# Twelve matmuls on four banks ahead of the last x, and another order of SyncE and GpSimd in one batch, in a fused attention + GELU MLP kernel

## Chip, cores, metric

One core of a Trainium2 chip. The metric is device microseconds of one execution; medians of several executions are quoted.

## The reference, cut

```python
B, H, S, D = 8, 8, 576, 64
scores = q @ k.T / sqrt(D);  cum = cumsum(log(clip(f, 1e-4, 1)))
scores = where(causal, -1e9, scores + cum[:, None] - cum[None, :])
attn   = softmax(scores) @ v                    # (B, H, S, D)
x      = attn.transpose(0, 2, 1, 3).reshape(B * S, 512)
out    = gelu(x @ w_in) @ w_out                 # w_in 512x2048, w_out 2048x512, float32 out
```

## The kernel before

The kernel runs batch by batch. In the attention of batch b (b >= 2) TensorE interleaves score tiles (`scores`), the attend matmuls of the head pair before (`av`) and steps of the second GEMM of batch b-1 (`take(fill, n)`). A step is "n" (one matmul of 128 rows) or "r" (two of 64 rows that run side by side). Each head pair's x is normalized on VectorE and transposed into xT by a DMA that SyncE issues (`x_dma`). The first GEMM of the batch then contracts over xT in four parts `kt`, one for each head pair; `kt = 3` needs the last x, which comes last.

```python
PLAN_1 = [(0, "m", 14*"r" + 2*"n"), (1, "m", 14*"r" + 2*"n"),
          (2, "m", 14*"r" + 2*"n"), (3, "s", 6*"r" + 10*"n")]     # second GEMM of batch 1, run in batch 2
FILL   = [[7,6,3,3], [1,3,3,2], [1,3,3,3], [1,3,3,3], [6]]        # steps taken after each score tile
FILL_2 = [[8,8,8,8], [8,8,4,4], [4,4,4,4], [4,4,4,4], [6]]        # the same for batch 2

def attention(b):
    ...
    for i in range(HP):                       # head pairs
        for t in range(4):                    # score tiles: matmuls, exp on ScalarE, masks on GpSimd
            scores(b, i, t)
            take(fill, counts[i][t])
            if i and t == 1:
                av(i - 1)                     # attend + normalize
                x_dma(b, i - 1)               # SyncE: transpose x -> xT
            if t == 1 and i == 0:
                load_v(b + 1)                 # SyncE: 5 DMAs into v_sb, once its last reader is done
            if b > 2 and t == 0 and i < 2:
                transpose_dma(b + 1, 4 * i, 4 * i + 4)
            if b == 2 and t == 1 and i == 1:
                transpose_dma(3, 0, 4)        # SyncE: q and k of the next batch
                transpose_dma(3, 4, 8)
    take(fill, counts[HP][0])
    av(HP - 1)
    x_dma(b, HP - 1)
    take(fill, 999)

    pss = [gemm1(b, ffb, (0, 1)) for ffb in range(2)]       # 4 matmuls
    for ffb in range(2):
        gemm1(b, ffb, (2,), pss[ffb])                       # 2
    pss.append(gemm1(b, 2, (0, 1, 2), spare()))             # 3: nine ahead of the last x
    for ffb in range(3):
        gemm1(b, ffb, (3,), pss[ffb])
    gemm1(b, 3, range(4), spare())
    ...
# in the rest of the first GEMM of batch 1: GpSimd computes vw = v * w for the pairs of batch 2
    if late == gap - 2:
        weigh_v(b + 1, at)                    # two instructions, about 1.4 us on GpSimd
```

The softmax here doesn't subtract the row's maximum and nothing guards it: scores larger than these inputs give would overflow.

## Time and profile before

| | before |
|---|---|
| median, first three executions | 346.34 us |
| median of six, with the later ones | 345.51 us (344.77 to 346.74) |
| profiled execution | 345.78 us, span 343.7 us |
| TensorE busy | 97% of the span |
| undisturbed first GEMM of a batch | 64 matmuls in 13.81 us |

The span is what the trace covers; the time of the execution is some 2 us longer. The prediction shows the lines that bound the kernel. How to read them: the chain lists the work that ended last, so where it leaves TensorE, TensorE stood.

### The profile page before, as it was taken

The numbers are of one execution on the slowest core, as the hardware profiler recorded it, in microseconds if no ns is written. First come the engines' busy times: TensorE is split into PE (matmuls) and PEld (weight loads), VectorE is DVE, ScalarE is ACT, GpSimd is POOL, SyncE is SP. The second block draws the span as 40 slices with busy tenths as digits, with TensorE's granted clock in tenths as the row PEclk, the third lists the DMA queues.
The fourth block names the chain that finished last, engine by engine and source line by source line (L and its number), as shares of the span: only waits on it lengthen the run. The fifth ranks groups of instructions, "written<-read, shape, count | busy, mean of one in ns | idle before, by whom it ended". The sixth has DMA issues, their size and how long they took to land.

```text
span 343.7 us, 7855 instructions
## 1 busy us (share of the span) xinstructions
PE 332.7 (97%) x3180; PEld 172.4 (50%) x3180; DVE 183.1 (53%) x417; ACT 210.4 (61%) x296; POOL 125.4 (36%) x256
## 2 busy tenths in 40 slices
PE   7899999999998999999999999999999999999995
PEld 3574555445553456445644465446544554444443
DVE  5660455943357934796469646975497551020011
ACT  5986786773743687378737873687568765504600
POOL 8391572219333334443436243714450430000000
PEclk9999999999999999999999999999999999999999
DMA  8999999989996799769973998299910131011013
GB/s 117 177 158 191 208 180 137 167 174 144 220 174 171 111 166 191 152 85 158 212 162 42 174 194 175 45 177 201 180 44 2 52 101 50 0 63 62 0 34 90
DMA packets 104628, 44.18 MB, mean 129 GB/s; under 512 B 83408, under 2 KB 100048, under 8 KB 104592
## 3 DMA queue, kind: packets, MB, share of 16 engines
q1 hardware_dynamic: 87296, 29.52, 44.2%
q0 software_dynamic: 16896, 13.63, 27.0%
q8 instruction: 25, 0.41, 0.5%
q10 hardware_dynamic: 400, 0.52, 0.4%
q14 instruction: 11, 0.09, 0.1%
HBM read 36.85 MB, written 9.44 MB: 135 GB/s over the span
## 4 chain that ended last, share of the span: by engine, by line
PE 88%; DMA 4%; DVE 2%; POOL 2%; ACT 2%; issue 1%; SPq 0%; POOLq 0%; ACTq 0%
PE ps L375 34%; PE ps L469 26%; PE o L320 8%; PE ps L411 8%; PE s L289 7%; DMA xT<-x 2%; PE ps L504 2%; ACT e L299 2%; DMA k<-in_k_dram 2%; POOL q L107 1%; PE ps_f L206 1%; DVE x L334 1%; POOL k L107 1%; PE ps_x L353 1%; DVE r L333 0%
## 5 line engine op out<-in xcount | busy, mean ns | idle before, releaser
L395 ACT ACTIVATE g<-ps 128x512 bf16<-128x512 f32 x144 | 83.4, 598 | 83.4 <-PE ps L375 82.9
L299 ACT ACTIVATE e<-s 128x896 bf16<-128x896 f32 (+2 forms) x128 | 101.2, 836 | 28.5 <-PE s L289 26.8
L375 PE MATMUL ps<-xT,w_in_sb 128*128 128x512 bf16 x512 | 113.3, 379 | 1.9 <-DMA xT<-x 1.8
L469 PE MATMUL ps<-w_out_sb,g 64*128 64x512 bf16 (+1 forms) x744 | 109.2, 377 | 0.0
L375 PEld LDWEIGHTS <-w_in_sb 128*128 128x128 bf16 x576 | 55.9, 98 | 70.2 <-issue 5.1
L301 POOL TENSOR_SCALAR_AFFINE_SELECT e<-e 128x256 bf16<-128x256 bf16 (+1 forms) x135 | 49.4, 384 | 94.6 <-ACT e L299 94.3
L469 PEld LDWEIGHTS <-g 64*128 64x128 bf16 (+1 forms) x744 | 41.7, 94 | 41.7 <-issue 11.9
L260 POOL TENSOR_TENSOR vw<-v_sb,wT 128x640 bf16<-128x640 f32 x31 | 39.9, 1288 | 34.2 <-DMA v_sb<-in_v_dram 24.7
L289 PE MATMUL s<-qT,kT 64*128 64x320 bf16 (+4 forms) x384 | 45.8, 276 | 3.4 <-ACT e L299 2.7
L477 DVE COPY ot<-ps 128x512 f32<-128x512 f32 x26 | 18.0, 691 | 48.0 <-PE ps L469 48.0
L244 DVE COPY kT<-tk 64x288 bf16<-64x288 bf16 x96 | 42.1, 438 | 1.6
L244 DVE COPY qT<-tq 64x288 bf16<-64x288 bf16 x96 | 38.9, 405 | 1.4
L320 PEld LDWEIGHTS <-e 128*128 128x128 bf16 x960 | 34.8, 98 | 5.8 <-issue 0.6
L320 PE MATMUL o<-vw,e 128*128 128x65 bf16 x960 | 36.9, 194 | 0.3 <-POOL e L301 0.2
L334 DVE TENSOR_TENSOR x<-o,r 128x320 bf16<-128x320 f32 x64 | 31.4, 491 | 2.2
L420 DVE COPY ot<-ps 128x512 f32<-128x512 f32 (+2 forms) x9 | 5.7, 632 | 48.9 <-PE ps L411 48.9
L289 PEld LDWEIGHTS <-kT 64*128 64x128 bf16 x384 | 19.5, 94 | 23.1 <-issue 9.7
L411 PE MATMUL ps<-w_out_sb,g 128*128 128x512 bf16 (+2 forms) x144 | 28.0, 355 | 0.0
L333 DVE RECIPROCAL r<-o 128x5 f32<-128x5 f32 x64 | 12.1, 189 | 25.0 <-PE o L320 24.9
L411 PEld LDWEIGHTS <-g 128*128 128x128 bf16 x144 | 13.5, 98 | 14.5
L479 DVE TENSOR_TENSOR ot<-ot,ps 128x512 f32<-128x512 f32 x26 | 17.8, 686 | 1.4
L375 PE MATMUL ps<-tails,w_in_sb 128*128 128x512 bf16 x64 | 14.4, 378 | 0.0
(64 smaller groups left out, 139.6 us busy)
## 6 DMA issues: line engine op xcount, KB each, us to landing
out_dram<-ot SPq DMA_DIRECT2D x32, 256.0 KB, 2.5
v_sb<-in_v_dram SPq DMA_DIRECT2D x24, 256.0 KB, 5.1
q<-in_q_dram POOLq DMA_DIRECT2D x6, 576.0 KB, 6.2
k<-in_k_dram POOLq DMA_DIRECT2D x6, 576.0 KB, 8.6
v_sb<-in_v_dram SPq DMA_DIRECT2D x22, 128.0 KB, 5.4
w_in_sb<-in_moe_w_in_dram POOLq DMA_DIRECT2D x4, 512.0 KB, 7.1
w_out_sb<-in_moe_w_out_dram POOLq DMA_DIRECT2D x4, 512.0 KB, 8.4
q<-in_q_dram POOLq DMA_DIRECT2D x4, 144.0 KB, 4.6
```

The lines of the kernel that those rows point to most:

```text
L244: nc.vector.tensor_copy(rows[:, odd], src[odd * D : (odd + 1) * D, 2 * i + h].rearrange("d j p -> d p j"),)
L260: eng.tensor_tensor(vw_of[b][:, hs, :, 0:D], v_sb[:, hs, :, :], w.unsqueeze(3).to_broadcast([P, 2, NBLK, D]), Alu.mult,)
L289: nc.tensor.matmul(to, *ab, start=half < 0, stop=half == 1 or not masked)
L299: nc.scalar.activation(et[:, :, z:c], st[:, :, z:c], Act.Exp, scale=scale)
L301: nc.gpsimd.affine_select(out=et[:, :, c0 + z : c0 + P], in_=et[:, :, c0 + z : c0 + P], compare_op=Alu.is_ge, fill=0.0, base=z, pattern=[[ ...
L320: nc.tensor.matmul(o[:, m, :], e_of[b, i, t][:, h, c : c + P], vw_of[b][:, 2 * i + h, n, :], start=(n == 0), stop=(n == m),)
L334: nc.vector.tensor_tensor(x_of[b, i][:, :, h, :], o[:, :, 0:D], r.unsqueeze(2).to_broadcast([P, NBLK, D]), Alu.mult,)
L375: nc.tensor.matmul(ps, w_in_sb[:, kt, ffb * P : (ffb + 1) * P], src[:, kt, 0:TC], start=(kt == 0), stop=(kt == n_dm - 1),)
L395: nc.scalar.activation(g_of[c][ffb], ps, Act.Gelu)
L411: nc.tensor.matmul(pss[ts][:, c0:c1], g_of[c][kt][:, ts * P : (ts + 1) * P], w_out_sb[:, kt, c0:c1], start=(kt == 0), stop=(kt == n_ff - 1),)
L469: nc.tensor.matmul(banks[r], g_of[c][kt][rows, ts * P : (ts + 1) * P], w_out_sb[rows, kt, :], start=kt == (steps.index("r") if r else 0), ...
L477: nc.vector.tensor_copy(ot, banks[1])
```

## The change

Three intents. First, every opening of the first GEMM in batches 2 to 7 gets more work that doesn't need the last x: twelve matmuls on four banks (each tile of the first GEMM adds up its four parts in one bank) in place of nine on three, and one second-GEMM step (two in batch 2) moves behind the last attend. Second, in batch 2 the q/k transposes of heads 4 to 7 go behind the last x in SyncE's queue, and two of the four products of v go behind the masks of the first head pair on GpSimd, with the next v load behind them. Third, the plan of the second GEMM that runs in batch 2 ends in whole steps only. The core of the diff:

```diff
-        (2, "m", 14 * "r" + 2 * "n"),
-        (3, "s", 6 * "r" + 10 * "n"),
+        (2, "m", 12 * "r" + 4 * "n"),
+        (3, "s", 16 * "n"),
...
-    FILL = [..., [6]];  FILL_2 = [..., [6]]
+    FILL = [..., [5]];  FILL_2 = [..., [4]]
...
-                if t == 1 and i == 0:
+                if b == 2 and (i, t) == (0, 3):
+                    weigh_v(b, 2)
+                    weigh_v(b, 3)
+                if i == 0 and t == (3 if b == 2 else 1):
                     load_v(b + 1)
...
                     transpose_dma(3, 0, 4)
-                    transpose_dma(3, 4, 8)
...
         x_dma(b, HP - 1)
+        take(fill, 4)
+        if b == 2:
+            transpose_dma(3, 4, 8)
         take(fill, 999)
...
-        pss.append(gemm1(b, 2, (0, 1, 2), spare()))
-        for ffb in range(3):
+        pss += [gemm1(b, ffb, (0, 1, 2), spare()) for ffb in (2, 3)]
+        for ffb in range(4):
             gemm1(b, ffb, (3,), pss[ffb])
-        gemm1(b, 3, range(4), spare())
+        more = s_psum.tile([P, 2, 512], FP32, tag="s", name="ps1")
+        gemm1(b, 4, ps=more[:, 0, :])
...
-                if late == gap - 2:
+                if late == gap - 2 and (b > 1 or at < 2):
                     weigh_v(b + 1, at)
```

(Cut: the copy-out of a tile without "r" steps, one VectorE copy in place of a copy and an add, and the numbering of the later tiles.)

More of the change, by code (lines that the diff above doesn't have):

```diff
@@ L465, in gemm2_rows @@
             for kt, step in enumerate(steps):
-                last = kt == steps.rindex("r")
+                last = kt == steps.rfind("r")
                 for r in range(2 if step == "r" else 1):
@@ L475, in gemm2_rows @@
                     )
-                if kt == n_ff - 1 if held == "s" else last:
+                if "r" in steps and (kt == n_ff - 1 if held == "s" else last):
                     nc.vector.tensor_copy(ot, banks[1])
                 if kt == n_ff - 1:
-                    nc.vector.tensor_tensor(ot, ot, banks[0], Alu.add)
+                    if "r" in steps:
+                        nc.vector.tensor_tensor(ot, ot, banks[0], Alu.add)
+                    else:
+                        nc.vector.tensor_copy(ot, banks[0])
                     store(c, ts, ot)
@@ L616, in gemm1_begin @@
         gelu(b, 3, pss[3])
-    FILL = [[7, 6, 3, 3], [1, 3, 3, 2], [1, 3, 3, 3], [1, 3, 3, 3], [6]]
-    FILL_2 = [[8, 8, 8, 8], [8, 8, 4, 4], [4, 4, 4, 4], [4, 4, 4, 4], [6]]
+    FILL = [[7, 6, 3, 3], [1, 3, 3, 2], [1, 3, 3, 3], [1, 3, 3, 3], [5]]
+    FILL_2 = [[8, 8, 8, 8], [8, 8, 4, 4], [4, 4, 4, 4], [4, 4, 4, 4], [4]]
     FILL_1 = [[0, 0, 0, 0], [0, 0, 0, 0], [2, 2, 2, 2], [2, 2, 2, 2]]
@@ L716 @@
             x_tail(0)
-        for ffb in range(4, n_ff):
-            gemm1(b, ffb, ps=spare() if b > 1 and ffb in (6, 7) else None)
+        for ffb in range(4 if b < 2 else 5, n_ff):
+            gemm1(b, ffb, ps=spare() if b > 1 and ffb in (7, 8) else None)
             if b == 0:
@@ L729 @@
             elif b + 1 < B:
-                first, gap = (5, 3) if b == 1 else (0, 4)
+                first, gap = (5, 3) if b == 1 else (1, 4)
                 at, late = divmod(ffb - first, gap)
```

## The prediction

> **What bounds the kernel now.** I read the page's busy shares first, then the chain that ended last, then the waits of TensorE, then the timeline around each place where that chain leaves TensorE. Page, part 1 (engine, busy us, share, instructions):
>
> ```profile
> PE 332.7 (97%) x3180; PEld 172.4 (50%) x3180; DVE 183.1 (53%) x417; ACT 210.4 (61%) x296; POOL 125.4 (36%) x256
> ```
>
> Only TensorE is near its span, and its clock row shows 9 in all 40 slices, so no throttle plays. A busy share says nothing on headroom where matmuls overlap, so the pitch matters. The chain in order of time (start us, length us, what) shows three openings of the first GEMM (L375), 64 matmuls each:
>
> ```profile
> 105.76 2.60 DMA xT<-x
> 108.40 12.03 PE ps L375 x55
> ...
> 142.01 13.81 PE ps L375 x64
> ...
> 176.18 3.40 DMA xT<-x
> 179.61 12.03 PE ps L375 x55
> ...
> 212.68 2.60 DMA xT<-x
> 215.32 12.03 PE ps L375 x55
> ...
> 248.93 13.81 PE ps L375 x64
> ```
>
> An undisturbed batch (3, 6, 7) is one piece of 64 matmuls in 13.81 us: 215.8 ns each. In batches 2, 4 and 5 the chain passes through the DMA transpose that brings x into xT, and only 55 matmuls follow it: the nine that can run without the last x were done, and TensorE stood. The list of TensorE's waits makes that the only sizeable one after batch 1:
>
> ```profile
> PE s L289 <- ACT e L299: 2.7, 7, 0.5
> PE ps L375 <- DMA xT<-x: 1.8, 4, 1.2
> ```
>
> (total us, times, longest. The first lies in the first two batches, which the change leaves alone.) The 1.8 understates it, since a matmul's modelled end (379 ns) overlaps the next; I work with starts. TensorE at the opening of batch 2:
>
> ```profile
> 104.52 0.38 PE L375 MATMUL ps<-xT,w_in_sb 128*128 128x512 bf16 x1
> 105.12 0.81 PE L375 MATMUL ps<-xT,w_in_sb 128*128 128x512 bf16 x3 [0.22 <-DMA xT<-x]
> 107.08 3.21 PE L375 MATMUL ps<-xT,w_in_sb 128*128 128x512 bf16 x13 [1.15 <-DMA xT<-x]
> ```
>
> Nine matmuls from 104.52 at 0.2158 end at 106.46; the tenth began at 108.40 (chain). **Batch 2 loses 1.94 us**: 0.38 before the second matmul (x of head pair 1), 1.31 before the fifth (pair 2), 0.24 before the tenth (pair 3). In batch 4 the first starts at 177.24, so the tenth could start at 179.18 and did at 179.61: **0.43 us**. Batch 5: 213.06, 215.00, 215.32: **0.32 us**. Together 2.69 us.
>
> Why is batch 2 different? SyncE's own timeline (start, length of the issue, what):
>
> ```profile
> 82.67 9.11 SPq L119 DMA_DIRECT2D v_sb<-in_v_dram  x5
> 91.83 1.09 SPq L484 DMA_DIRECT2D out_dram<-ot  x2
> 93.11 1.28 SPq L359 DMA_TRANSPOSE xT<-x  x1
> 94.47 1.36 SPq L230 DMA_TRANSPOSE tq<-q  x1
> 95.92 1.66 SPq L230 DMA_TRANSPOSE tk<-k  x1
> 97.64 2.13 SPq L230 DMA_TRANSPOSE tq<-q  x1
> 99.82 1.69 SPq L230 DMA_TRANSPOSE tk<-k  x1
> 101.61 0.76 SPq L484 DMA_DIRECT2D out_dram<-ot  x1
> 102.47 1.23 SPq L359 DMA_TRANSPOSE xT<-x  x1
> ```
>
> SyncE issues in order. The load of the next v occupies it for 9 us, four q/k transposes of the next batch for 7 more, and x of pair 1, whose last normalize ended near 91.7 (its attend matmuls ended near 90.6, plus about 1.1 us on VectorE as in the later batches), is not issued before 102.47. Pairs 2 and 3 follow at 104.42. So it is the queue's order that is late, not the data.
>
> **What the Trainium skill says.** "TensorE: Matmul & The Clock Gate", section "Wait — 56ns, not 53.3ns?": warm matmuls of 512 columns start 215.7 ns apart. The trace agrees (13.81 us / 64 = 215.8). "Perfetto Trace Analysis", section "Summary: the profiler window per engine type": the window of a DMA issued by SyncE covers the lock wait, descriptor generation and the semaphore push, not the data movement. So the lengths above are time for which the queue is held, and the landing comes on top; the DMA list gives 2.7 us median from issue to landing for x. "DMA: Bandwidth & Descriptors", section "Issuing engines are not separate DMA queues": queues of all issuers run on the same 16 engines and interleave. The trace agrees: the v load held SyncE for 9.11 us while q and k were still loading, against 4.93 us in batch 3, after k had landed. "TensorEngine Tiling (Array Packing)", section "Key Properties": switching the tiling mode drains TensorE. In batch 2, 18 steps of the second GEMM with two changes of mode took 104.52 - 100.43 = 4.09 us against 18 x 0.2158 = 3.88, so about 0.1 us a change.
>
> **Part 1: twelve matmuls and one more step.** The opening goes from nine matmuls ahead of the last x to twelve: 3 x 0.2158 = 0.65 us more cover in batches 2 to 7, by putting the fourth tile of d_ff ahead too. In batches 3 to 7 the attend of the last pair moves one second-GEMM step earlier and that step runs after it: 0.22 us more. Cover grows by 0.86 us, the work stays the same. Against needs of 0.43 (batch 4) and 0.32 (batch 5) both waits should go: **0.75 us** saved. In batches 3, 6 and 7 there is nothing to win.
>
> **Part 2: SyncE in batch 2.** Two of the four q/k transposes (the 2.13 and 1.69 us, 3.9 with gaps) go behind the x of pair 3. Against that, the v load is emitted two score tiles later and waits for the two products of v on GpSimd, which now come after the masks of pair 0. The last exponential of pair 0 ends at 82.77 + 0.81 = 83.6; its mask takes 0.4 at most, to 84.0; the two products 1.28 + 0.23 each with gaps, to about 86.9. So the v load starts near 86.9 instead of 82.67. By then q and k, issued at 78.4, should be nearly in: in batch 3 they were issued at 113.20 and k had landed by 123.3, 10 us, hence 88.5 here. I take 5.5 us for the five issues (4.93 when alone): free at 92.4, 0.6 later than now. From there by the row lengths above: one store 0.5, x of pair 0 1.3, two transposes 3.1, a store 0.8, x of pair 1 issued at about 98.3, landed 101.0; a store, x of pair 2 issued near 100.2, landed 102.9; x of pair 3 once its normalize ends.
> The attend of pair 3 starts two steps earlier (0.43 us), so that end is 101.52 - 0.43 = 101.1; issued by 102 it lands by 104.7. The first GEMM starts near 104.3 and needs pair 1 at 104.5, pair 2 at 105.2 and pair 3 at 104.3 + 12 x 0.2158 = 106.9. All in time: **1.94 us** saved.
>
> **Part 3: plan of batch 2.** The last tile is now sixteen whole steps and the tile before it ends in four, so after the attend there is no change of mode until the first GEMM: two changes less, **0.2 us**. VectorE saves one copy of 0.69 us, off the path.
>
> **Part 4: the banks.** A fifth tile takes a bank pair of the score pool. Its earlier user is read by the exponential that ended by 98.2 in batch 2, long before. Four tiles now finish within 0.86 us, and ScalarE needs 0.60 us each: done 2.65 us after the first. The sixth tile takes the first tile's bank 1.73 us after that end, free since 0.6; the ninth comes back to the fourth's bank at 4.3, free since 2.65. No wait added.
>
> Sum: 0.75 + 1.94 + 0.2 = 2.9 us; 346.34 - 2.9 = 343.4. The profiled run, whose waits I sized, took 345.78, a little under the median, so the median run may have lost somewhat more: I say **343.3**.
>
> **Rivals.** (a) SyncE stays late in batch 2. If the v load again takes 9.1 us from 86.9 it frees the queue at 96.0, pair 1 is issued near 101.9, lands at 104.6, pair 2 at 106.5 against 105.2, pair 3 near 107.9. About 1.3 us of the 1.94 comes back: 344.7. For it: the transfers before were saturated (200 to 250 GB/s from 84 to 90). Against: q and k have 4 us more to themselves. (b) A new wait takes the place: the attend of pair 0 now has two products of v ahead of it in the program. If they held it to 86.9 instead of 84.3, 2.6 us would be lost and nothing gained overall: 346. Against: in batch 0 the first attend ran at 17.25 while the products of pairs 1 to 3 lay at 17.12 to 22, so waits go by the part of the tile. Also, the last attend, 0.2 to 0.4 us earlier, could meet its masks: in batch 3 the last ends at 138.16 and the attend starts at 138.74, so 0.36 us is left. (c) The openings were hidden anyway: no, the chain passes through them with TensorE idle. (d) More than 2%, 6.9 us: there isn't that much idle TensorE left in the changed stretch.
>
> **Range and chances.** All hidden and the median's surplus too gives about 342; rival (a) with a late transfer somewhere gives 345. Runs of before spread over 2 us. So 341.9 to 345.2. Faster than 339.4 would need twice the waits that exist; slower than 353.3 a stall that nothing here shows: 1% each.
>
> **What would show it.** Right: first GEMM of batches 2 to 7 as unbroken pieces of 64 in the chain, no x transpose in the chain there, the wait for xT near 0, x of pair 1 in batch 2 issued before 100. Step 2 is wrong if the v load of batch 2 holds SyncE for over 8 us, or if the second to tenth matmul still wait. Part 4 is wrong if the first GEMM waits for ScalarE; rival (b) if an attend waits for GpSimd.

## The result

The changed kernel took **343.09 us** (342.81 to 343.89, 6 executions) against 345.51 us. The ratio was 0.9928, 95% interval 0.9904 to 0.9952. Ratios here are the mean time of one kernel's runs over that of the other's in the same rounds, so not quite the ratio of the medians. Executions over 1.5% slower than the fastest of the same kernel are left out of the means. The profiled execution has a span of 340.9 us, 2.8 less than before.

The chain of the changed kernel, openings of batches 2 to 7 (start us, length us, what):

```profile
104.55 13.81 PE ps L375 x64
...
139.94 13.81 PE ps L375 x64
...
175.34 13.81 PE ps L375 x64
...
210.73 13.81 PE ps L375 x64
...
246.12 13.81 PE ps L375 x64
...
281.52 13.81 PE ps L375 x64
```

All six are whole, and the wait of the first GEMM for xT is gone from TensorE's list. SyncE's timeline in batch 2 of the changed kernel (start, length of the issue, what):

```profile
83.92 7.53 SPq L119 DMA_DIRECT2D v_sb<-in_v_dram  x5
91.55 0.57 SPq L487 DMA_DIRECT2D out_dram<-ot  x1
92.30 1.27 SPq L359 DMA_TRANSPOSE xT<-x  x1
93.66 1.40 SPq L230 DMA_TRANSPOSE tq<-q  x1
95.15 1.65 SPq L230 DMA_TRANSPOSE tk<-k  x1
96.89 0.78 SPq L487 DMA_DIRECT2D out_dram<-ot  x1
97.77 1.80 SPq L359 DMA_TRANSPOSE xT<-x  x1
99.66 0.53 SPq L487 DMA_DIRECT2D out_dram<-ot  x1
100.29 2.55 SPq L359 DMA_TRANSPOSE xT<-x  x2
```

x of pair 1 is issued at 97.77 in place of 102.47, and pairs 2 and 3 from 100.29 in place of 104.42.

**A ledger of the two traces.** I cut each trace at the first score of batch 2, at each first matmul of a first GEMM and at the first matmul after it.

| stretch, us | before | after | saved |
|---|---|---|---|
| start to the first score of batch 2 | 72.40 | 72.51 | -0.11 |
| batch 2, first score to first GEMM | 32.12 | 31.88 | 0.24 |
| opening of batch 2, over an undisturbed 13.91 | 1.94 | 0 | 1.94 |
| opening of batch 4 | 0.43 | 0 | 0.43 |
| opening of batch 5 | 0.31 | 0 | 0.31 |

(13.91 is the 64 matmuls and the change to the scores.) The rows add to 2.8 us, the whole difference of the spans. The attention stretches of batches 3 to 7 are 21.47 to 21.49 us in both.

### The profile page after: what moved, and what is told of

It is laid out like the page before. It is cut to its first block, busy times and chain, and to the rows that moved or that the text cites. A ratio compares the mean times of both kernels' runs of the same rounds, so it can differ in the third digit from the quotient of the medians.

```text
span 340.9 us, 7841 instructions
## 1 busy us (share of the span) xinstructions
PE 331.2 (97%) x3172; PEld 172.8 (51%) x3172; DVE 184.5 (54%) x416; ACT 209.1 (61%) x296; POOL 125.3 (37%) x256
## 4 chain that ended last, share of the span: by engine, by line
PE 91%; POOL 2%; ACT 2%; DMA 2%; DVE 1%; issue 1%; POOLq 0%; ACTq 0%
PE ps L375 36%; PE ps L469 27%; PE o L320 9%; PE ps L411 8%; PE s L289 7%; PE ps L507 2%; ACT e L299 2%; DMA k<-in_k_dram 2%; POOL q L107 1%; PE ps_f L206 1%; DVE x L334 1%; POOL k L107 1%; PE ps_x L353 1%; DVE r L333 0%; DVE qT L213 0%
## 5 line engine op out<-in xcount | busy, mean ns | idle before, releaser
L395 ACT ACTIVATE g<-ps 128x512 bf16<-128x512 f32 x144 | 82.1, 601 | 81.8 <-PE ps L375 81.8
L301 POOL TENSOR_SCALAR_AFFINE_SELECT e<-e 128x256 bf16<-128x256 bf16 (+1 forms) x135 | 49.3, 384 | 97.9 <-ACT e L299 97.6
L244 DVE COPY qT<-tq 64x288 bf16<-64x288 bf16 x96 | 43.1, 449 | 1.4
L244 DVE COPY kT<-tk 64x288 bf16<-64x288 bf16 x96 | 39.7, 413 | 1.6
L477 DVE COPY ot<-ps 128x512 f32<-128x512 f32 x25 | 17.3, 691 | 42.1 <-PE ps L469 42.1
```

Source lines behind the costliest of these rows:

```text
L244: nc.vector.tensor_copy(rows[:, odd], src[odd * D : (odd + 1) * D, 2 * i + h].rearrange("d j p -> d p j"),)
L301: nc.gpsimd.affine_select(out=et[:, :, c0 + z : c0 + P], in_=et[:, :, c0 + z : c0 + P], compare_op=Alu.is_ge, fill=0.0, base=z, pattern=[[ ...
L395: nc.scalar.activation(g_of[c][ffb], ps, Act.Gelu)
L477: nc.vector.tensor_copy(ot, banks[1])
```

## The experiments

Each kernel was timed in five rounds beside the kernel before. Medians of before moved by 0.4 us, so ratios are compared. For each profiled execution the same cuts give this table: "stage" is batch 2 from first score to first GEMM, "opening" what each first GEMM took over the undisturbed one (13.91 us, 13.81 in batch 7), "v" when the first product of v of batch 2 began on GpSimd, which shows when that v had landed. (In e2 and e5 the profile names a matmul as what released that product. That matmul comes later in the program and cannot be it; I read the v load there as well.)

| kernel | median us | ratio to before (95%) | v | stage | opening of 2 | of 3 to 7 |
|---|---|---|---|---|---|---|
| before | 345.51 | 1 | 75.63 | 32.12 | 1.94 | 0.43 (4), 0.31 (5) |
| changed | 343.09 | 0.9928 (0.9904 to 0.9952) | 75.21 | 31.88 | 0 | 0 |
| e1 opening only | 345.57 | 1.0004 (0.9970 to 1.0037) | 77.32 | 33.82 | 0.76 | 0.49 (4) |
| e2 order only | 344.60 | 0.9973 (0.9946 to 1.0000) | 77.28 | 32.10 | 0 | 1.07 (4) |
| e3 transposes only | 344.38 | 0.9975 (0.9948 to 1.0002) | 74.49 | 32.09 | 0 | 1.33 (4) |
| e4 changed, old plan | 343.94 | 0.9964 (0.9940 to 0.9987) | 75.43 | 32.09 | 0 | 0.67 (4) |
| e5 changed, nine | 343.43 | 0.9942 (0.9912 to 0.9972) | 77.12 | 31.87 | 0 | 0.24 (5), 0.28 (6) |
| e6 changed, six | 344.75 | 0.9973 (0.9941 to 1.0006) | 75.75 | 31.87 | 0 | 1.58 in all, 1.12 of it (5) |
| e7 changed, fifteen | 343.33 | 0.9941 (0.9911 to 0.9972) | 74.99 | 31.87 | 0 | 0.06 (6) |
| e8 plan only | 345.98 | 1.0010 (0.9976 to 1.0044) | 77.06 | 33.22 | 1.44 | 0.30 (5) |
| e9 before, product doubled | 346.18 | 1.0010 (0.9975 to 1.0045) | 74.73 | 32.45 | 0.84 | 0.14 (3), 0.80 (4) |
| e10 changed, product doubled | 343.78 | 0.9937 (0.9907 to 0.9966) | 78.01 | 32.31 | 0 | 0 |
| e11 transposes, product doubled | 345.90 | 1.0000 (0.9966 to 1.0034) | 75.53 | 33.23 | 0 | 1.05 (4) |
| e12 v part only | 347.48 | 1.0040 (1.0009 to 1.0071) | 76.57 | 32.09 | 4.20 | 1.09 (4) |

### e1: the longer opening alone

The changed kernel with the plan, the counts of batch 2 and the order of SyncE and GpSimd put back:

```diff
-    (2, "m", 12*"r" + 4*"n"), (3, "s", 16*"n")      # and FILL_2 ending in [4], and both new order pieces
+    (2, "m", 14*"r" + 2*"n"), (3, "s", 6*"r" + 10*"n")
```

> The longer openings of batches 2 to 7 alone, with the order and plan of batch 2 as before. My theory: batches 4 and 5 lose nothing any more (0.75 us saved), batch 2 still waits 0.38 us for x of pair 1 and 1.31 us for pair 2, because those stand before the fifth matmul whatever the opening's length; only its 0.24 us before the last x goes. So about 1.0 us less than before. Rival (the longer opening is what repaired batch 2 too): about 2.7 us less, and no wait in batch 2.

Measured: ratio 1.0004, no gain. The rival is refuted: batch 2 still waits at its opening. But the expected 1.0 us did not appear either. Batch 5 lost nothing, as expected, but batch 4 still lost 0.49 us with twelve matmuls ahead of the last x, which took 4.32 us from issue to landing. And the trace shows a wait that I had not foreseen. TensorE at the first attend of batch 2 in e1:

```profile
84.90 0.23 PE L320 MATMUL o<-vw,e 128*128 128x65 bf16 x2 [0.38 <-POOL e L301]
85.86 1.33 PE L320 MATMUL o<-vw,e 128*128 128x65 bf16 x28 [0.73 <-POOL e L301]
```

and GpSimd ahead of it, also e1:

```profile
77.32 1.28 POOL L260 TENSOR_TENSOR vw<-v_sb,wT 128x640 bf16<-128x640 f32 x1 [15.29 <-DMA v_sb<-in_v_dram]
...
84.44 2.69 POOL L301 TENSOR_SCALAR_AFFINE_SELECT e<-e 128x256 bf16<-128x256 bf16 x8
```

In the old order the masks of pair 0 (L301) stand behind all four products of v and two DMA issues. Those can't start before v has landed, at 77.32 here. So the masks come at 84.44 and the attend waits for them: the stage takes 33.82 us in place of 32.12, 1.70 us more. In the profile of before the same two lines are

```profile
75.63 1.28 POOL L260 TENSOR_TENSOR vw<-v_sb,wT 128x640 bf16<-128x640 f32 x1 [13.60 <-DMA v_sb<-in_v_dram]
...
82.75 2.68 POOL L301 TENSOR_SCALAR_AFFINE_SELECT e<-e 128x256 bf16<-128x256 bf16 x8
```

with the attend at 84.34: just in time. The masks of e1 came 1.69 us later and the stage took 1.70 us more, so the masks of before had next to no slack. Part of the 1.7 us reappears as a smaller opening wait (0.76), because SyncE's queue had that time to catch up.

### e2 and e3: the order alone, and of it the transposes alone

e2 is the kernel before with both order pieces of the diff; e3 has only the transposes' move:

```diff
                     transpose_dma(3, 0, 4)
-                    transpose_dma(3, 4, 8)
...
+        take(fill, 4)
+        if b == 2:
+            transpose_dma(3, 4, 8)
```

> The order of SyncE and GpSimd in batch 2 alone, with nine matmuls in every opening and the old plan. My theory: the 1.94 us of batch 2 go, the waits of batches 4 and 5 stay (0.75 us as sized, though they change from execution to execution): about 1.9 us less than before. Rival (longer opening is the cure): batch 2 still waits over 1 us.

> Only the two q/k transposes moved behind the last x of batch 2; the products of v and the load of the next v stay where they were. My theory: x of pair 1 is then issued near 98 and pair 2 near 100, so the same 1.9 us less as with the whole new order; the v load's move gives nothing to the time. Rival (the v load's place is what frees SyncE): 1 us or less is saved and pair 1 or 2 is still late.

Both lost nothing at the opening of batch 2, with nine matmuls ahead of the last x. So the order, not the longer opening, mends batch 2, and of the order it is the transposes' move. In time both gained about 0.9 us of the 1.9 expected (0.9973 and 0.9975, with intervals that just reach 1). In their profiled executions batch 4 lost 1.07 and 1.33 us, since its last x took 4.03 and 4.29 us from issue to landing, against the usual 2.6. The chain of e3 there (start, length to the landing, what):

```profile
174.19 4.29 DMA xT<-x
```

The fixed openings of nine leave that uncovered; twelve cover 2.59 us and would not cover it either (0.49 lost in e1, 0.67 in e4). Whether this alone makes up the missing 1.0 us in the median is not shown.

The two traces also differ in when v landed. In e2 v landed late, as in e1, yet:

```profile
77.28 1.28 POOL L260 TENSOR_TENSOR vw<-v_sb,wT 128x640 bf16<-128x640 f32 x1 [14.71 <-PE ps L504]
```

```profile
84.86 1.11 PE L320 MATMUL o<-vw,e 128*128 128x65 bf16 x30
```

(GpSimd, then TensorE, of e2.) The attend runs without a wait, stage 32.10, since two products no longer stand ahead of the masks. In e3 v happened to land at 74.49, so its old GpSimd order cost nothing.

### e4 and e8: the plan of batch 2

e4 is the changed kernel with the old plan and `FILL_2` ending in 6; e8 is the kernel before with the new plan and `FILL_2` ending in 4.

> The changed kernel with only the old plan and step counts of batch 2's second GEMM put back. My theory: two changes of tiling mode come back, first GEMM of batch 2 starts 0.2 us later, nothing waits for x: 0.2 us more than the changed kernel, 2.5 us less than before. Rival (the attend moved two steps earlier was needed to have the last x in time): a wait for the last x of batch 2 in the trace and 0.5 us or more lost.

> The kernel before with only the new plan and step counts of batch 2's second GEMM. The second GEMM of batch 2 ends 0.2 us sooner, but its x of pairs 1 and 2 is held up in SyncE's queue, whose times do not depend on it. My theory: TensorE waits 0.2 us longer there and the time is that of before, within 0.2 us. Rival (the parts add wherever they stand): 0.2 us less, with the waits of batch 2 unchanged.

e4's stage took 32.09 us against 31.88: **0.21 us**, as expected for two changes of tiling mode, and no wait for x in batch 2. The time was 0.9964, more than 0.2 us worse than the changed kernel. The intervals overlap, but the trace has a reason for it: batch 4 lost 0.67 us, with twelve matmuls, to a landing of 4.33 us. That goes with the plan, as the part on the prediction shows below. e8 gained nothing (1.0010), as my theory has it, but a gain of 0.2 us lies within its interval. Its trace had v landing late and a stage of 33.22, so it is inconclusive on the rival. Its batch 4 lost nothing, with nine matmuls.

### e5, e6, e7: nine, six and fifteen matmuls in the changed kernel

```diff
-        pss += [gemm1(b, ffb, (0, 1, 2), spare()) for ffb in (2, 3)]      # twelve
+        pss.append(gemm1(b, 2, (0, 1, 2), spare()))                       # e5: nine, as before
+        # e6: neither line: six;  e7: a fifth tile's first three as well: fifteen
```

> The changed kernel with nine matmuls ahead of the last x in batches 2 to 7 (one more second-GEMM step after the attend is kept). In the changed kernel's trace the last x landed 2.0, 1.5, 2.6, 1.4 and 1.6 us after the start of the first GEMM in batches 3 to 7, and before its start in batch 2. Nine matmuls cover 1.94 us. My theory: only batch 5 waits, 0.7 us; 0.3 to 0.8 us more than the changed kernel. Rival (the openings' length no longer matters once the order is mended): no difference and no wait for x.

> The same with six matmuls ahead of the last x, which cover 1.29 us. My theory: each batch loses what its landing exceeds 1.29 us: 0.7, 0.2, 1.3, 0.1 and 0.3 us in batches 3 to 7, 2.6 us in all over the changed kernel, back to the time of before. Rival (no dependence on the opening): no difference.

> The same with fifteen matmuls on five banks ahead of the last x, 3.24 us of cover. Nothing waits for x in the changed kernel's trace, so within 0.2 us of it; batch 5, where the last x landed 2.6 us after the start and twelve cover 2.59, would only gain in executions in which it comes later. If instead five tiles that end together overload ScalarE, a wait of the first GEMM for ScalarE appears and the time rises.

Six 344.75, nine 343.43, fifteen 343.33. The openings lost 1.58, 0.52 and 0.06 us in the traces. Each loss goes with the landing of that execution: in e6 the copy on GpSimd that waits for the last x began 2.59 us after the first GEMM in batch 5 and 1.45 to 1.68 us in batches 3, 4, 6 and 7. Six matmuls cover 6 x 0.2158 = 1.29, so batch 5 should lose up to 1.3 us and lost 1.12; the others lost 0.04 to 0.28. I expected 2.6 us for six from the changed kernel's landings. That was too much: the x of e6's batch 3 came 0.54 us earlier, and that copy starts 0.1 us or so after the matmul could. Fifteen shows no gain over twelve (0.9941 against 0.9928), and no wait for ScalarE appears. Beyond nine, the steps are below what five rounds resolve: in its one trace nine loses half a microsecond.

### e9 to e12: is it the masks?

The first product of v of batch 2 is computed twice, which holds GpSimd about 1.4 us longer with the same result:

```diff
                     weigh_v(b + 1, at)
+                    if b == 1 and at == 0:
+                        weigh_v(b + 1, at)
```

in the kernel before (e9), in the changed one (e10) and in e3 (e11). e12 is the kernel before with only the v part of the new order: products 2 and 3 behind the masks of pair 0, the next v load behind them.

> The kernel before with the first product of v of batch 2 computed twice on GpSimd (same result, 1.4 us more there), as if the v load had landed 1.4 us later. Found in two of the traces: where that v lands near 77 instead of 75.5, the masks of pair 0, which stand behind all four products of v, come late and the first attend of batch 2 waits 1.1 to 1.5 us on GpSimd. Theory: this wait appears here, 1.3 us or more; x of batch 2 comes 1.4 us later too, so about 1.0 to 1.5 us more than before. Rival (GpSimd has slack there): no wait on GpSimd, same time.

> The same doubling in the changed kernel, where the masks of pair 0 stand ahead of the last two products of v. Theory: no wait on GpSimd; SyncE's v load starts 1.4 us later, which the openings still cover: within 0.3 us of the changed kernel (343.1). Rival (the change only moved the wait to SyncE): x of batch 2 late again, 0.5 us or more lost.

> The same doubling in the kernel with only the two q/k transposes moved. Theory: the first attend of batch 2 waits 1.3 us or more on GpSimd, and nothing in that batch's opening absorbs it: 1.0 to 1.5 us more than that kernel without the doubling (344.4), so near 345.7. Rival (the transposes' move alone protects batch 2): 344.4.

> The kernel before with only the products of v put behind the masks of pair 0 and the next v load put behind them; the q/k transposes stay ahead of x. Theory: the first attend never waits, but x of pairs 1 and 2 still comes when SyncE's queue lets it, near 107 in both cases, so the opening of batch 2 loses 1.5 us or more and the time is that of before within 0.4 us. Rival (this part is worth something by itself): 0.7 us or more less than before.

e10 against e11: 343.78 and 345.90. e11, with the old GpSimd order, shows the wait for the masks (0.7 us in the list) and a stage of 33.23, 1.1 us over e3's. e10's stage grew by only 0.43 to 32.31, although its v landed at 78.01, the latest of all, and its product was doubled on top. So the new order protects, up to a limit that e10 touches: I had expected no wait on GpSimd there, and its masks came late enough to cost those 0.43 us. (The two kernels differ in more than this order, so the stage compares them, not the time.) e9 missed: its v landed at 74.73, so the doubling cost the stage only 0.33 us, and the time did not move (1.0010).

e12 refutes what I expected of it. It is slower than before by 0.4% (0.1 to 0.7). The attend didn't wait (stage 32.09), but SyncE's v load began at 85.30 in place of 82.67, with the four transposes still ahead of x, so pair 1's x was issued at 103.26. TensorE in e12:

```profile
105.90 0.81 PE L375 MATMUL ps<-xT,w_in_sb 128*128 128x512 bf16 x3 [1.03 <-DMA xT<-x]
107.87 3.57 PE L375 MATMUL ps<-xT,w_in_sb 128*128 128x512 bf16 x8 [1.16 <-DMA xT<-x]
```

The starts give idle stretches of 1.19 us (from 104.49 + 0.22) and 1.32 us (from 105.90 + 0.65). The eight matmuls from 107.87 then take about 3.4 us in place of 1.7: the clock was halved. The windows of e12 (stretch, its length, busy us and instructions of PE, PEld, DVE, ACT, POOL, then clock, DMA share, GB/s):

```profile
108.00:110.00 2.00, 2.00 (x6) 0.66 (x5) 1.88 (x7) 0.00 (x0) 0.81 (x2) 0.50 0.86 256
110.00:112.00 2.00, 2.00 (x8) 0.82 (x7) 1.99 (x2) 1.38 (x3) 2.00 (x3) 0.67 0.18 67
```

1.19 + 1.32 + 1.7 is the 4.20 us in the table. The Trainium skill, "TensorE: Matmul & The Clock Gate", section "HAM oscillation — how this bites in real kernels", gives as the rule to keep gaps of idle TensorE under about 3.4 us. Here two gaps of 1.2 and 1.3 us, 0.65 us apart, were followed by half clock. A single gap of 1.33 us (batch 4 of e3) was not. This was the slowest of e12's six executions (348.37 us, clock 0.995), and one more has that clock (348.11). Without these two e12's mean is still 1.0 us above before's, in place of 1.4, so the halving is at most a part of why e12 is slower.

## Why the prediction was right

It said 343.3 us in 341.9 to 345.2; 343.09 came. Point by point:

- **Opening of batch 2, 1.94 us: right.** The ledger shows it gone. e2 and e3 show that the transposes' move does it; e1 shows that the longer opening doesn't.
- **Openings of batches 4 and 5, 0.75 us: right in the trace** (0.43 + 0.31), **but only batch 5 for the reason given.** What an opening loses is the time at which the last x lands, counted from the first matmul, less the cover: in batch 4, 2.34 - 1.94 in before (0.43 lost), 3.04 - 2.59 in e1 (0.49), 3.24 - 1.94 in e3 (1.33); and in batch 5 of e6, 2.38 - 1.29 (1.12). In the changed kernel the last x of batch 5 landed at 2.45, which twelve cover and nine would not. That of batch 4 landed at 1.30: nine would have done. The sizes are those of one execution of each kernel.
- **What batch 4 goes with is the plan of batch 2**, which I had not foreseen. From issue to landing its last x took 3.40 to 4.33 us in all eight traces with the old plan (before, e1 to e4, e9, e11, e12) and 2.57 to 2.60 in all six with the new one (changed, e5 to e8, e10). The packets in the traces suggest why. In the eight, one 16 KB packet of the queue that the profile calls "instruction" started 0.6 to 2.2 us after the issue, and the transpose's last 4-byte packets ended only after it. In the six it started 3.6 to 3.8 us after the issue, when x had landed. The new plan has eight matmuls fewer, so what is fetched as the program goes on may come later. That the packet holds x up is not tested by a run of its own.
- **Mode changes, 0.2 us: right**, 0.24 in the ledger, 0.21 from e4. The stages in which the attend didn't wait agree: 32.09 to 32.10 us with the old plan (e2, e3, e4, e12), 31.87 to 31.88 with the new one (changed, e5, e6, e7).
- **Banks, no wait: right.** With four and even five tiles ending together (e7) no wait for ScalarE shows.
- **SyncE's times in batch 2: the result right, the steps off.** I took the exponential that ended at 83.6 for the last of pair 0; it belongs to pair 1. The masks of pair 0 ended at 81.27 in the changed kernel, and the v load began at 83.92, not 86.9. Its five issues took 7.53 us, not 5.5, but not the 9.1 of rival (a). The two errors nearly cancel: the queue was free at 91.45, not 92.4, and pair 1's x was issued at 97.77, where I said 98.3. (Also, pair 1's normalize in before ended at 92.07, not 91.7; nothing hangs on it.)
- **What failed: the worth of the GpSimd part.** I counted it as a delay of the v load with a risk (rival b) that the changed kernel's attend would wait for the two products. It does not: in e2 the attend began at 84.86, while the last product ran from 84.72 to 85.99. It is the kernel before whose first attend waits, in executions in which v lands late; the profile that I read had v landing at 75.63, just early enough. Late landings with the old order and nothing doubled cost 1.7 and 1.3 us (e1, e8: stages 33.82 and, with the new plan, 33.22 against 31.88). With the new order they cost nothing (e2, e5 and e12, landings of 76.57 to 77.28).
- **The sum**, 2.9 us from 346.34: the trace gives 2.8, the ratio 2.5, the medians 2.4. The three-run median that I started from was 0.8 us above that of six. From 345.51 the same sum gives 342.6. So the prediction's 343.3 was this close partly by luck: it started too high and took off too much.

How much of the median gain belongs to each part is open. Alone, the opening gave nothing measurable, the order 0.9 us, the v part of it a loss of 1.4 us (0.4% of 345.9). Together they gave 2.5. The landing of v falls differently in each trace, that of batch 4's last x goes with the plan, and five rounds don't separate parts below a microsecond. With one trace of each kernel, it is open how often v lands late.

## What to carry to other kernels

Where TensorE is 97% busy, count lost time from the starts at each stage's opening, against an undisturbed stage; the list of waits understates it. Read an in-order queue (SyncE's issues, GpSimd) as a schedule: an item that nobody needs soon must not stand ahead of one that TensorE waits for. And one profile is one execution: slack of next to nothing in it, as the masks had here, is a wait in the next one, so part of a change's worth can be protection that the profile doesn't show. When a loss goes away, compare it over all the variants before crediting the part that was meant for it: batch 4's loss went with the plan, not with the longer opening.

## What the Trainium skill lacked or had wrong

- "TensorE: Matmul & The Clock Gate": the rule in the section named above is for idle gaps over about 3.4 us; another section speaks of shorter idling between groups of matmuls, without a length. In e12 gaps of 1.19 and 1.32 us, 0.65 us apart, were followed by a granted clock of 0.50 and about 1.7 us lost on top.
- "TensorEngine Tiling (Array Packing)": it says that a change of tiling mode drains the engine, without a figure. Here two changes less saved 0.21 to 0.24 us, so about 0.1 us each.
- "DMA: Bandwidth & Descriptors": no spread is given for a transpose from SBUF to SBUF. Over the 14 traces the same x transpose took 2.5 us at least and 2.7 to 3.1 in the median from issue to landing, with a slowest one of 4.3 to 4.9 in each.
- The same page calls a sequencer's issue time usually small relative to the DMA itself. In the trace of before (the loads for batches 2 to 7) a single issue of a v load held SyncE for 0.4 to 5.4 us and the five of one load for 4.7 to 11.8, against 3.7 to 11.5 us from issue to landing of one. That queue, not the transfer of x, was what TensorE waited for in batch 2.
- No page on DMA says what a packet of the "instruction" queue does to a transfer beside it. Here the last x of batch 4 took 3.40 to 4.33 us in the eight traces in which one fell into it and 2.57 to 2.60 in the other six; that one causes the other is not shown.
